# Float64 weights to float32: sign kept by a one-source mask on 16-bit halves

## The chip, the cores and the metric

The kernel runs on one core of one Trainium2 chip. The metric is the device time of one execution in microseconds (us), lower is better. Engines are named as in the profile: PE (matrix engine), PEld (its weight loads), DVE (vector engine), ACT (scalar engine), POOL (GpSimd), SP (issues the DMAs).

## What is computed

```python
A = sm(q, k_lm); Bm = sm(q_lm, k_lm); C = sm(q_lm, k)     # landmark attention, 4 batches x 8 heads
Z = Bm.T / (norm1 * norminf + 1e-6)
for _ in range(6): Z = 2 * Z - Z @ Bm @ Z
x = A @ Z @ C @ v                                         # 2304 tokens x 512
h = x @ w_in;  x = (h * sigmoid(h)) @ w_out               # first MLP, 512 -> 2048 -> 512
xn = x / rms(x) * rms_g                                   # second MLP, 512 -> 1536 -> 512
return (silu(xn @ w_gate) * (xn @ w_val)) @ w_out2
```

The five weight matrices arrive as float64 and are used as pairs of float32 values (a leading part and a remainder), so that each product is three matmuls.

## The kernel before

The program has two large parts. In the first, four batches go through attention and the first MLP; in the second, six blocks of 384 tokens, taken in pairs, go through the second MLP, whose weights have been prepared during the first part and kept in DRAM.

A float64 value is two 32-bit words. The high word holds sign, 11 exponent bits and 20 mantissa bits, the low word the other 32 mantissa bits. A float32 needs the sign, 8 exponent bits and 23 mantissa bits, so 20 mantissa bits come from the high word and 3 from the top of the low word. `to_f32` does this in four instructions per piece (512 or 1024 values in each of 128 partitions):

- L164, ACT: reads the high word as a float32, takes its absolute value and scales it by 2^-112, which moves the exponent; result in `c`.
- L165, ACT: reads the upper 16 bits of the low word and turns them into the three missing bits, an integer 0 to 7, written over the low word as int32.
- L169, DVE: ANDs the high word with the sign bit and ORs the three bits in; result over the low word.
- L171, DVE: shifts `c` left by 3 and ORs the low word in; `c` is now the float32.

It is a generator that yields ahead of each DVE instruction, so callers can spread it. Raw tiles are called `winr` (`w_in`), `wor` (`w_out`) and `r_v`, `r_g`, `r_o` (second MLP); results are `win`, `wos` and `c_v`, `c_g`, `c_o`. Results `wos`, every other `c_` tile and the evacuated sums `e` share one pool of four buffers (`stage`); L164 is the instruction that needs such a buffer, L165 needs only the raw tile. There are 8 `win` loads (those for the first 1024 columns in two pieces of 512 each), 16 `wor` loads and 36 loads for the second MLP, 64 pieces of each instruction in all.

After that a result of `w_out` is split into leading part and remainder (`split`, L145 to L148; the leading part of the first four by DVE on L147, later by ACT on L145, the remainder by POOL on L148).

The order of the work is made by a scheduler from program order and priorities. At the start the attention of batch 0 for its two groups of heads runs step by step, and the string `CONV` says how many conversion steps are let in behind each attention step. When attention is done, `wprime` (L428 to L431) multiplies the attention's small matrices with `win` and splits the result (`wp`); `moe1_h` (L587, L590) multiplies that with the queries' side and applies silu; `moe1_out` (L599) multiplies with `w_out` into four accumulators `a`; `moe1_sum` (L609, L611) moves the accumulators out to `e`, and the next half of the batch takes their place. From step 24 of the MLP loop on, `conversion` works through the second MLP's weights. Each engine runs its own list strictly in order.

Of the kernel before, what the change touches and what calls it, by code (L numbers as in the profile page):

```python
# [13 lines left out]
U16 = mybir.dt.uint16  # L14
AF = mybir.ActivationFunctionType
ALU = mybir.AluOpType
# [44 lines left out]
def nystrom_moe_kernel(ctx: ExitStack, tc: tile.TileContext, q, k, v, w_in, w_out, w_gate, w_val, w_out2, rms_g, out):  # L61
    nc = tc.nc
    PE, DVE, ACT, POOL, SP = nc.tensor, nc.vector, nc.scalar, nc.gpsimd, nc.sync
# [90 lines left out]
    def to_f32(c, raw, act=1024, dve=1024):  # L154


        n = c.shape[1]
        w = raw.rearrange("p (f t) -> p f t", t=2)
        lo, hi = w[:, :, 0], w[:, :, 1]
        lo16 = raw.bitcast(U16).rearrange("p (f t) -> p f t", t=4)[:, :, 1]  # L160
        ci = c.bitcast(I32)
        for x in range(0, n, act):
            y = slice(x, min(n, x + act))
            ACT.activation(c[:, y], hi[:, y].bitcast(F32), AF.Abs, scale=2.0 ** -112)  # L164
            ACT.activation(lo[:, y], lo16[:, y], AF.Copy, scale=2.0 ** -13, bias=2.0 ** -14 - 0.5)  # L165
        for x in range(0, n, dve):
            y = slice(x, min(n, x + dve))
            yield
            DVE.scalar_tensor_tensor(out=lo[:, y], in0=hi[:, y], scalar=-0x80000000, in1=lo[:, y], op0=ALU.bitwise_and, op1=ALU.bitwise_or)  # L169
            yield  # L170
            DVE.scalar_tensor_tensor(out=ci[:, y], in0=ci[:, y], scalar=3, in1=lo[:, y], op0=ALU.logical_shift_left, op1=ALU.bitwise_or)  # L171

    def finish(gn):
        for _ in gn:
# [11 lines left out]
    def load_win(n, g):  # L186
        raw = wslot(f"winr_{g}_{n}", [P, 2, 1024], I32)
        SP.dma_start(out=raw, in_=win_v[g, n].rearrange("c p f -> p c f"))
        yield
        t = nslot(2 * n + g, f"win_{g}_{n}", [P, 2, 512])  # L190
        size = (512, 512) if n < 2 else (1024, 1024)
        yield from to_f32(t.rearrange("p c f -> p (c f)"), raw.rearrange("p c f -> p (c f)"), *size)
        win_t[g, n] = t

    def load_wout(f):
        raw = wslot(f"wor_{f}", [P, 2 * DM], I32, f"o{f}", 1)
        SP.dma_start(out=raw, in_=w_out_v[f * P:(f + 1) * P, :])
        yield
        s = stage(f"wos_{f}")
        yield from to_f32(s, raw)  # L200
        t = wslot(f"wo_{f}", [P, 2, DM], F32R, f"o{f}", 1)
        split(t, s, lo=POOL, hi=DVE if f in range(EARLY) else ACT)
        wo_t[f] = t
# [255 lines left out]
    def conversion():  # L459

        raws, gens, outs = {}, {}, {}

        def load(n, f, what):
            raw = raws[n] = nslot(4 + n % 3, f"r_{what}_{f}", [P, 1024], I32)
            if what == "o":
                SP.dma_start(out=raw, in_=w_out2_v[f * P:(f + 1) * P, :])
            else:
                src = w_gate_v if what == "g" else w_val_v
                SP.dma_start(out=raw.rearrange("p (k f) -> p k f", k=KD), in_=src[:, f * 2 * P:(f + 1) * 2 * P].rearrange("(k p) f -> p k f", p=P))

        def start(n, f, what):
            outs[n] = stage(f"c_{what}_{f}") if n % 2 else nslot(7, f"c_{what}_{f}", [P, 512])
            gens[n] = to_f32(outs[n], raws[n])
            next(gens[n])

        def go_on(n):
            next(gens[n], None)

        def store(n, f, what):
            j = "vgo".index(what)  # L480
            SP.dma_start(out=w2d[f, :, j * 512:(j + 1) * 512], in_=outs[n])

        jobs = []
        for n, (f, what) in enumerate((f, what) for f in PRE + list(range(PRE_N, NF2)) for what in "vgo"):
            jobs += [(4 * n + 1, load, n, f, what), (4 * n + 9, start, n, f, what), (4 * n + 10, go_on, n), (4 * n + 11, go_on, n), (4 * n + 15, store, n, f, what)]
        return in_time(jobs)
# [368 lines left out]
    t = 0  # L855
# [203 lines left out]
```

## Time and profile before

| what | us |
|---|---|
| three runs | 896.09, 898.78, 899.06 |
| median | 898.78 |
| profiled execution, first to last instruction (its span) | 890.5 |
| PE busy in it | 831.2 |
| DVE busy | 538.4 |
| ACT busy | 453.0 |
| POOL busy | 206.8 |

The profile gives the span of the profiled execution and no separate time for it; the three runs lie 5.6 to 8.6 us above the span. A row of the stretch view gives the busy time of each engine between two moments of the span, then the clock granted to PE as a share of full speed (1.00 is the 2.4 GHz level, 0.50 the 1.2 GHz level). A row of the timeline gives start, length, engine, line, operation, output<-input, shape, and in brackets the idle time before it with what ended it.

### The profile page before, as it was taken

The numbers are of one execution on the slowest core, as the hardware profiler recorded it, in microseconds if no ns is written. First come the engines' busy times: TensorE is split into PE (matmuls) and PEld (weight loads), VectorE is DVE, ScalarE is ACT, GpSimd is POOL, SyncE is SP. The second block draws the span as 40 slices with busy tenths as digits, with TensorE's granted clock in tenths as the row PEclk, the third lists the DMA queues.
The fourth block names the chain that finished last, engine by engine and source line by source line (L and its number), as shares of the span: only waits on it lengthen the run. The fifth ranks groups of instructions, "written<-read, shape, count | busy, mean of one in ns | idle before, by whom it ended". The sixth has DMA issues, their size and how long they took to land.

```text
span 890.5 us, 14692 instructions
## 1 busy us (share of the span) xinstructions
PE 831.2 (93%) x5436; PEld 747.6 (84%) x5436; DVE 538.4 (60%) x1070; ACT 453.0 (51%) x926; POOL 206.8 (23%) x232
## 2 busy tenths in 40 slices
PE   4578999999989999999899999999999999999996
PEld 3447788688868888899899988999989999999995
DVE  5988978448954665668873568843468534333332
ACT  2858784468446955657363445533445433222322
POOL 5257563223322333372650002400000000000000
PEclk9659999999999999999999999999999999999998
DMA  9774935883868556979668545759655556655553
GB/s 326 284 287 145 307 111 186 285 269 108 275 201 286 157 159 240 361 276 290 242 241 313 211 168 191 248 213 318 249 213 211 206 201 240 230 200 194 205 194 71
DMA packets 72584, 202.82 MB, mean 228 GB/s; under 512 B 6592, under 2 KB 34240, under 8 KB 68544
## 3 DMA queue, kind: packets, MB, share of 16 engines
q1 hardware_dynamic: 72512, 201.88, 64.7%
q8 instruction: 43, 0.70, 0.3%
q14 instruction: 29, 0.24, 0.1%
HBM read 149.29 MB, written 52.56 MB: 227 GB/s over the span
## 4 chain that ended last, share of the span: by engine, by line
PE 55%; DVE 9%; DMA 9%; ACT 8%; issue 4%; POOL 1%; SPq 0%; DVEq 0%; ACTq 0%; POOLq 0%
PE ga L737 16%; PE o L811 16%; PE gc L737 8%; PE a L599 7%; PE gb L737 4%; PE h L587 3%; DMA r_g<-in_moe_w_gate_dram 2%; DMA w7d<-w7p 2%; DMA wod<-wop 2%; DMA r_o<-in_moe_w_out_dram 1%; DMA r_v<-in_moe_w_val_dram 1%; DVE w7p L148 1%; DVE kT L217 1%; DVE qT L217 1%; DMA win<-wind 1%
## 5 line engine op out<-in xcount | busy, mean ns | idle before, releaser
L599 PE MATMUL a<-hl,wo 128*128 128x288 f32 x1536 | 228.2, 297 | 10.8 <-DVE e L611 6.7
L599 PEld LDWEIGHTS a<-hl,wo 128*128 128x128 f32 x1536 | 212.6, 190 | 14.7 <-DVE e L611 4.8
L811 PE MATMUL o<-oc,u 128*128 128x512 f32 x648 | 178.1, 393 | 0.0
L737 PE MATMUL ga<-x,w 128*128 128x384 f32 x840 | 170.6, 337 | 1.1 <-ACT a L217 1.0
L737 PEld LDWEIGHTS ga<-x,w 128*128 128x128 f32 x840 | 150.5, 188 | 14.2 <-ACT a L217 2.3
L587 PE MATMUL h<-at,wp 128*128 128x288 f32 x768 | 134.4, 310 | 8.1 <-DVE wp L431 4.1
L587 PEld LDWEIGHTS h<-at,wp 128*128 128x128 f32 x768 | 111.3, 194 | 32.8 <-issue 10.7
L811 PEld LDWEIGHTS o<-oc,u 128*128 128x128 f32 x648 | 119.3, 188 | 13.0 <-DVE u L148 0.3
L148 POOL TENSOR_TENSOR hl<-s,hl 128x288 fp32r<-128x288 f32 x86 | 78.0, 912 | 155.4 <-ACT hl L145 107.4
L217 DVE TENSOR_TENSOR v<-u,gc 128x384 f32<-128x384 f32 x72 | 39.7, 552 | 119.5 <-PE gc L737 116.1
L737 PE MATMUL gc<-x,w 128*128 128x384 f32 x420 | 84.6, 336 | 0.0
L590 ACT ACTIVATE s<-h 128x288 f32<-128x288 f32 x128 | 52.0, 409 | 50.8 <-PE h L587 35.8
L737 PEld LDWEIGHTS gc<-x,w 128*128 128x128 f32 x420 | 74.6, 188 | 3.1
L217 DVE TENSOR_TENSOR u<-z,v 128x384 f32<-128x384 f32 x72 | 40.4, 561 | 50.5 <-ACT z L217 49.5
L217 ACT COPY u<-ga 128x384 f32<-128x384 f32 x72 | 34.5, 480 | 70.3 <-PE ga L737 70.0
L145 ACT CAST u<-u 128x384 fp32r<-128x384 f32 x72 | 36.9, 513 | 65.3 <-DVE u L217 65.2
L148 DVE TENSOR_TENSOR u<-u,u 128x384 fp32r<-128x384 f32 x72 | 40.1, 557 | 28.3 <-ACT u L145 28.0
L502 POOL TENSOR_TENSOR t<-fw 128x256 f32<-128x256 f32 x24 | 23.7, 1005 | 144.4 <-ACT x L701 82.8
L145 ACT CAST hl<-s 128x288 fp32r<-128x288 f32 x128 | 54.8, 433 | 2.4
L217 ACT ACTIVATE z<-ga 128x384 f32<-128x384 f32 x36 | 17.7, 492 | 73.2 <-PE ga L737 73.1
L737 PE MATMUL gb<-x,w 128*128 128x384 f32 x210 | 42.3, 336 | 0.9 <-DVE v L217 0.9
L737 PEld LDWEIGHTS gb<-x,w 128*128 128x128 f32 x210 | 36.7, 188 | 1.4 <-DVE v L217 1.2
(166 smaller groups left out, 1050.3 us busy)
## 6 DMA issues: line engine op xcount, KB each, us to landing
w<-w7d SPq DMA_DIRECT2D x31, 1792.0 KB, 7.3
oc<-wod SPq DMA_DIRECT2D x32, 512.0 KB, 8.0
win<-wind SPq DMA_DIRECT2D x20, 512.0 KB, 6.6
fw<-w2d SPq DMA_DIRECT2D x12, 768.0 KB, 6.8
winr<-in_moe_w_in_dram SPq DMA_DIRECT2D x8, 1024.0 KB, 10.7
wor<-in_moe_w_out_dram SPq DMA_DIRECT2D x16, 512.0 KB, 8.1
w7d<-w7p SPq DMA_DIRECT2D x16, 512.0 KB, 5.3
r_v<-in_moe_w_val_dram SPq DMA_DIRECT2D x12, 512.0 KB, 5.4
```

The costliest lines, as they stand in the source:

```text
L145: ACT.copy(dst[:, 0], src)
L148: lo.tensor_tensor(dst[:, 1], src, dst[:, 0].bitcast(F32), op=ALU.subtract)
L217: self.last = getattr(self.eng, name)(*args, **kw)
L502: POOL.tensor_tensor(t[:, to], x, y, op=ALU.subtract)
L587: PE.matmul(ph, w[:, x, fo:fo + P], a[:, y, tk], start=i == 0, stop=i == 5)
L590: ACT.activation(s, ph, AF.Silu)
L599: PE.matmul(acc[d], w[:, x, d * P:(d + 1) * P], hl[:, y], start=start and i == 0, stop=stop and i == 2)
L737: mm[0] = PE.matmul(acc, w7[:, x, o, kk], xs[:, y, kk], start=start and n == 0, stop=stop and n == 5, skip_group_check=True)
L811: PE.matmul(oacc[n], hls[j][:, x, t * P:(t + 1) * P], w[:, y], start=f == 0 and i == 0, stop=f == NF2 - 1 and i == 2)
```

## The change

The sign is no longer moved into the low word. L169 becomes a one-source instruction that masks the upper 16-bit half of the high word in place with 0x8000, so only the sign bit stays there. L165 writes its three bits as a 16-bit number into the lower half of the same high word. The high word then holds sign and three bits, and L171 ORs it in instead of the low word.

```diff
-        lo, hi = w[:, :, 0], w[:, :, 1]
-        lo16 = raw.bitcast(U16).rearrange("p (f t) -> p f t", t=4)[:, :, 1]
+        hi = w[:, :, 1]
+        q = raw.bitcast(U16).rearrange("p (f t) -> p f t", t=4)
...
             ACT.activation(c[:, y], hi[:, y].bitcast(F32), AF.Abs, scale=2.0 ** -112)
-            ACT.activation(lo[:, y], lo16[:, y], AF.Copy, scale=2.0 ** -13, bias=2.0 ** -14 - 0.5)
+            ACT.activation(q[:, y, 2], q[:, y, 1], AF.Copy, scale=2.0 ** -13, bias=2.0 ** -14 - 0.5)
...
-            DVE.scalar_tensor_tensor(out=lo[:, y], in0=hi[:, y], scalar=-0x80000000, in1=lo[:, y], op0=ALU.bitwise_and, op1=ALU.bitwise_or)
+            DVE.tensor_scalar(q[:, y, 3], q[:, y, 3], 0x8000, None, op0=ALU.bitwise_and)
...
-            DVE.scalar_tensor_tensor(out=ci[:, y], in0=ci[:, y], scalar=3, in1=lo[:, y], op0=ALU.logical_shift_left, op1=ALU.bitwise_or)
+            DVE.scalar_tensor_tensor(out=ci[:, y], in0=ci[:, y], scalar=3, in1=hi[:, y], op0=ALU.logical_shift_left, op1=ALU.bitwise_or)
```

Both L165 and L169 now overwrite what L164 reads. Before, L165 and L169 needed only the raw tile; now both stand behind L164. L169 no longer needs L165, and L171 needs all three.

The scheduler makes a new order of this. PE's list is the same but for three places where neighbouring matmuls change places. The other lists differ wherever a conversion stands. Three places follow.

First, ACT at the end of batch 0's attention, where the first `w_out` pieces are converted (`wor` raw, `wos` result, L430 the leading part of `wp`):

```order
-L165 ACTIVATE wor_4_561<-wor_4_561 128x512
-L165 ACTIVATE wor_5_563<-wor_5_563 128x512
-L165 ACTIVATE wor_6_565<-wor_6_565 128x512
-L165 ACTIVATE wor_7_567<-wor_7_567 128x512
 L430 CAST wp_0_0_532<-pw_0_0_0_533 128x512
 L164 ACTIVATE wos_4_573<-wor_4_561 128x512
-L165 ACTIVATE wor_8_581<-wor_8_581 128x512
+L165 ACTIVATE wor_4_561<-wor_4_561 128x512
 L430 CAST wp_0_0_532<-pw_0_0_1_534 128x512
 L164 ACTIVATE wos_5_583<-wor_5_563 128x512
-L165 ACTIVATE wor_9_591<-wor_9_591 128x512
+L165 ACTIVATE wor_5_563<-wor_5_563 128x512
```

The L165 of pieces 4 to 7 ran ahead of their L164; now each follows its own.

Second, DVE where the first half of batch 0 ends and its accumulators are moved out (L611; `kT` and `lm` belong to the attention of batch 1, `winr_3` and `win_3` are the last two `w_in` loads). Before:

```order
L169 SCALAR_TENSOR_TENSOR wor_680<-wor_680 128x512
L217 TENSOR_REDUCE kT_0_780<-kT_0_780 128x2x32
L169 SCALAR_TENSOR_TENSOR wor_778<-wor_778 128x512
L217 TENSOR_TENSOR lm_1_0_974<-kT_0_780,m_95 128x64 x2
L169 SCALAR_TENSOR_TENSOR winr_3_761<-winr_3_761 128x1024
L171 SCALAR_TENSOR_TENSOR win_3_1036<-win_3_1036,winr_3_761 128x1024
L611 COPY e_0_0_0_890<-a_0_0_0_656 128x288
L169 SCALAR_TENSOR_TENSOR winr_3_768<-winr_3_768 128x1024
L611 COPY e_0_0_2_896<-a_0_0_2_658 128x288
L171 SCALAR_TENSOR_TENSOR win_3_1041<-win_3_1041,winr_3_768 128x1024
```

The same place on DVE now:

```order
L217 TENSOR_TENSOR lm_0_930<-qT_0_730,m_95 128x64
L169 TENSOR_SCALAR winr_3_761<-winr_3_761 128x1024
L171 SCALAR_TENSOR_TENSOR win_3_1036<-win_3_1036,winr_3_761 128x1024
L611 COPY e_0_0_0_890<-a_0_0_0_656 128x288
L169 TENSOR_SCALAR winr_3_768<-winr_3_768 128x1024
L171 SCALAR_TENSOR_TENSOR win_3_1041<-win_3_1041,winr_3_768 128x1024
L611 COPY e_0_0_2_896<-a_0_0_2_658 128x288
L217 TENSOR_REDUCE kT_0_780<-kT_0_780 128x2x32
L431 TENSOR_TENSOR wp_2_912<-pw_2_0_913,wp_2_912 128x512
```

Two masks and the reduction of `kT` no longer stand ahead of the first L611; the last L171 now stands ahead of the second.

Third, ACT in the attention of batch 1, first group (`sa`, `bb`, `ec` are exponentials, `s` silu; each change between them loads a table). Before:

```order
L217 ACT_TABLE_LOAD
L217 ACTIVATE sa_0_1003<-sa_0_1003 128x576
L590 ACT_TABLE_LOAD
L590 ACTIVATE s_1_6_1070<-h_1_6_1063 128x288
L217 ACT_TABLE_LOAD
L217 ACTIVATE bb_0_1129,su_0_1130<-c_1_0_1055,nb_0_1088 128x32
```

The same place on ACT now:

```order
L217 ACT_TABLE_LOAD
L217 ACTIVATE sa_0_1003<-sa_0_1003 128x576
L217 ACTIVATE bb_0_1129,su_0_1130<-c_1_0_1055,nb_0_1088 128x32
L217 ACTIVATE ec_0_1128,su_0_1130<-c_1_0_1055,nb_0_1088 128x8x32
L217 ACTIVATE ec_0_1128,su_0_1130<-c_1_0_1054,nb_0_1088 128x10x32
L145 CAST wo_1051<-wos_1046 128x512
L590 ACT_TABLE_LOAD
L590 ACTIVATE s_1_6_1070<-h_1_6_1063 128x288
```

Silu no longer comes between the exponentials here, which takes out two loads; the second group of the same batch gains two, and the first group of batch 3 loses two (24 loads before, 22 now).

## Rows read from the trace of the kernel before

**Rows 1.** The page, parts 1 and 2: busy times, then tenths in 40 slices.

```profile
PE 831.2 (93%) x5436; PEld 747.6 (84%) x5436; DVE 538.4 (60%) x1070; ACT 453.0 (51%) x926; POOL 206.8 (23%) x232
...
PE   4578999999989999999899999999999999999996
...
PEclk9659999999999999999999999999999999999998
```

**Rows 2.** Stretches: length; PE, PEld, DVE, ACT, POOL busy (instructions); clock; DMA share; GB/s.

```profile
25.00:50.00 25.00, 16.40 (x152) 10.72 (x153) 24.57 (x74) 16.99 (x32) 6.61 (x6) 0.58 0.83 315
50.00:75.00 25.00, 20.39 (x118) 15.81 (x117) 18.69 (x23) 17.82 (x33) 17.90 (x14) 0.73 0.46 172
75.00:100.00 25.00, 21.22 (x149) 17.88 (x147) 24.28 (x30) 19.37 (x38) 14.41 (x12) 0.93 0.76 264
100.00:125.00 25.00, 22.15 (x203) 17.98 (x202) 21.13 (x51) 21.80 (x44) 13.47 (x13) 1.00 0.58 184
125.00:350.00 225.00, 214.47 (x1803) 187.84 (x1802) 143.81 (x353) 135.24 (x286) 68.42 (x76) 0.99 0.65 209
...
465.00:890.50 425.50, 415.69 (x2156) 384.01 (x2156) 204.72 (x381) 162.65 (x322) 14.53 (x13) 0.99 0.59 215
```

**Rows 3.** Lines L169, L147, L165: ns min/median/max; then who waited for L169.

```profile
L169 DVE SCALAR_TENSOR_TENSOR wor<-wor x16: 678/684/1794, 44.9 to 113.3; 128x512 int32<-128x512 int32 x16
...
  PEld h L587: 1.7, 1
...
L147 DVE CAST wo<-wos x4: 415/417/769, 46.9 to 54.0; 128x512 fp32r<-128x512 f32 x4
...
L165 ACT ACTIVATE wor<-wor x16: 646/672/719, 38.4 to 112.6; 128x512 int32<-128x512 uint16 x16
```

**Rows 4.** Timeline of DVE ahead of the first product of batch 0's MLP.

```profile
50.72 1.75 DVE L169 SCALAR_TENSOR_TENSOR wor<-wor 128x512 int32<-128x512 int32 x1
...
53.43 0.69 DVE L431 TENSOR_TENSOR wp<-pw,wp 128x512 fp32r<-128x512 f32 x1
54.04 0.77 DVE L147 CAST wo<-wos 128x512 fp32r<-128x512 f32 x1
```

**Rows 5.** Timeline of POOL in the same stretch.

```profile
50.33 1.59 POOL L148 TENSOR_TENSOR wo<-wos,wo 128x512 fp32r<-128x512 f32 x1 [1.62 <-ACT wor L165]
52.94 1.59 POOL L148 TENSOR_TENSOR wo<-wos,wo 128x512 fp32r<-128x512 f32 x1 [1.02 <-DVE wo L147]
```

**Rows 6.** Timeline of PE: its waits, and one undisturbed row for comparison.

```profile
38.79 1.19 PE L390 MATMUL pe<-rt,ebd 128*128 128x128 f32 x4 [1.23 <-DVE rt L217]
...
54.18 1.81 PE L587 MATMUL h<-at,wp 128*128 128x288 f32 x6 [3.30 <-DVE wp L431]
...
79.10 1.74 PE L599 MATMUL a<-hl,wo 128*128 128x288 f32 x12
...
89.22 2.59 PE L599 MATMUL a<-hl,wo 128*128 128x288 f32 x12 [2.94 <-DVE e L611]
...
110.16 1.06 PE L587 MATMUL h<-at,wp 128*128 128x288 f32 x6 [0.90 <-ACT s L590]
...
114.64 0.91 PE L369 MATMUL ct<-ident,ec 128*96 128x128 f32 x6 [1.35 <-ACT s L590]
...
149.34 1.84 PE L599 MATMUL a<-hl,wo 128*128 128x288 f32 x12 [1.37 <-DVE e L609]
```

**Rows 7.** Timeline of DVE where the first accumulators are moved out.

```profile
80.50 2.29 DVE L217 TENSOR_REDUCE kT<-kT 128x64 f32<-128x1152 f32 x1
...
85.74 1.21 DVE L169 SCALAR_TENSOR_TENSOR winr<-winr 128x1024 int32<-128x1024 int32 x1
...
88.72 0.44 DVE L611 COPY e<-a 128x288 f32<-128x288 f32 x1
```

**Rows 8.** Timeline of ACT: a wait for a stage buffer, and a table load.

```profile
56.61 0.67 ACT L164 ACTIVATE wos<-wor 128x512 f32<-128x512 f32 x1 [1.36 <-POOL wo L148]
...
108.40 1.28 ACT L590 ACT_TABLE_LOAD   x1
```

## The prediction, made before the changed kernel was run

> **What bounds the kernel now.** I read the page first, then the stretch view, then the timelines of the stretches where PE idles. PE is busy for 831.2 of 890.5 us [rows 1], so 59 us of idle time and the time lost at a low clock are all that a cheaper conversion can touch. In the second MLP, from 465 us on, PE works 415.69 of 425.5 us and no conversion runs there [rows 2]: nothing can change. From 125 to 350 us, where the 36 pieces of the second MLP's weights are converted, PE is idle 225 - 214.47 = 10.5 us with DVE and ACT each busy less than two thirds of the time [rows 2]. The dense losses are early: from 25 to 50 us DVE is busy 24.57 of 25 us and PE 16.40, at a granted clock of 0.58 [rows 2]. There DVE sets the pace: PE waits for DVE in the iterations of attention, as in the row with 1.23 us [rows 6], and the first product of the MLP waits 3.30 us for `wp` from L431 on DVE [rows 6]. A second loss stands at 89.22 us, where PE waits 2.94 us for the accumulators that L611 moves out on DVE [rows 6], and the clock over that stretch is 0.93 [rows 2]. A third lies at 110 to 115 us, 0.90 and 1.35 us of waiting for silu on ACT [rows 6].
>
> **The cost of the mask.** The two-source L169 takes 0.684 us for 512 values, and up to 1.794 us [rows 3]. The trace of before has no one-source pass on 16-bit halves. The bounds: the cast L147, one source in SBUF, 512 values, takes 0.417 us [rows 3]; a pass at the pace of L169 would take 0.684. I take 0.42, since L147 shares with the mask what L169 does not have: a single source in SBUF. So each piece of 512 saves 0.684 - 0.417 = 0.27 us, and one of 1024 about twice that. Below 0.417 I have no row; if it went lower still the gains below grow by at most as much again, which the low end of the range covers.
>
> The longest L169s are not slow arithmetic. The one at 50.72 us took 1.75 us while POOL worked from 50.33 to 51.92 [rows 4, 5], and the one-source L147 at 54.04 took 0.77 instead of 0.417 while POOL worked until 54.53 [rows 3, 4, 5]. So a mask started beside POOL waits too, and I give no gain for that wait. The Trainium skill, in "SBUF — State Buffer", section "SBUF: two separate sides", states the rule behind this: DVE and GpSimd hold a shared port pair for a whole instruction, and an instruction of DVE in a two-port mode is locked out as one with two SBUF sources is. It speaks against the hope that dropping a source frees DVE from POOL; the stretched L147 agrees. Were the mask free of it, the piece at 50.72 alone would save 1.75 - 0.42 = 1.3 us instead of 0.27.
>
> L165 keeps its 0.672 us [rows 3]: it already reads 16-bit numbers at that spacing, only the output changes its width. L164 and L171 stay. So ACT's work is the same and DVE loses 60 x 0.27 + 4 x 0.53 = 18 us of 538.4 [rows 1]; what counts is where.
>
> **Stretch up to the first product, 25 to 54 us.** Eleven L169 of 512 values stand in DVE's list there. At 0.27 each that is 2.9 us, and DVE is nearly never idle, so most of it moves L431 forward. I take off about 0.3 for one that stands in a gap where DVE waits for PE anyway, and 0.6 for the places where POOL's instruction, not the mask, ends the wait (rows 5 show two such POOL instructions of 1.59 us). That leaves 2.0 us earlier for the product at 54.18 [rows 6]. Bounds: 1.1 (the four masks of `wor` alone, if attention's own round trips through PE hide the others) and 2.9. New waits here: L171 now needs L165, but ACT has done the `winr` and first `wor` pieces two or more us before DVE comes to them, and the L165 that now follow the L164 of pieces 5 to 7 stand where ACT sits idle for a stage buffer, 1.36 us before the L164 at 56.61 [rows 8]. 0.67 fits into that. So I cost the new order of ACT at nothing here; if that cover were gone it would be 2 x 0.67 = 1.3 us on the way to the first silu.
>
> **The accumulators, 84 to 92 us.** Before, the first L611 at 88.72 stood behind a mask of 1.21 us at 85.74 and its L171, and these behind a reduction of 2.29 us and two other masks [rows 7]. PE waited 2.94 us, and the twelve matmuls after it took 2.59 instead of 1.74 us [rows 6]. The clock of 0.93 over 25 us is 1.75 us lost in all [rows 2]. So 4.7 us lie here. In the new list the reduction and two masks are gone from ahead of the first L611, 2.29 + 2 x 0.68 = 3.6 us of DVE work, but the second L611 stands behind a L171, which in turn needs ACT's last L165. I expect the first accumulator to come free about 3 us earlier and the third about 1.5 us earlier than now; PE needs the third after six matmuls. I take -1.5 us. Bounds: -4.7 (the wait and the slow clock both go; at 149.34 a wait of 1.37 us left the twelve matmuls at 1.84, close to 1.74 [rows 6]) and +3.0 (see the second rival).
>
> **Table loads, 100 to 130 us.** The first group of batch 1 loses two loads of 1.28 us [rows 8], against waits of 0.90 + 1.35 us for silu [rows 6]; the second group gains two. I take 0 for the pair, with bounds of 2.25 either way.
>
> **Second MLP's weights, 125 to 350 us.** 36 masks save 36 x 0.27 = 9.7 us of DVE, but PE waited directly for a L169 only 1.7 us in one place [rows 3]. L165 behind L164 makes each conversion a little longer from stage buffer to result, with loads far ahead. I take 0, bounds -1.7 and +1.7. After 350 us, 0.
>
> **Sum.** -2.0 - 1.5 + 0 + 0 = -3.5 us, so a span of 890.5 - 3.5 = 887.0. The three runs lie 5.6 to 8.6 us above the profiled span; against the median the same difference gives 898.78 - 3.5 = 895.3 us.
>
> **Rivals.**
> First, the early gain is eaten: PE comes 1 to 2 us earlier to the accumulators and waits that much longer there, since their release hangs on transfers and ACT. Then -2.0 + 1.5 = -0.5 is left, 898.3 us. For it: DVE is busy 24.28 of 25 us in that stretch [rows 2], so PE's earliness alone moves nothing. Against it: the list ahead of the first L611 is shorter.
>
> Second, slower: the second L611 stands behind a L171 that now waits for ACT's L165 of the last `winr` piece. Everything behind it on DVE is queued too: the reduction of `kT`, `wp` of the next columns, the exponentials' maxima; PE waits for the accumulator. If that L165 ends later than 88.7 us, where the first L611 stands now [rows 7], each us costs PE one. At 5 us late (about the present wait and the twelve slow matmuls behind it once more, 2.94 + 2.59) and with the early gain kept, the sum is -2.0 + 5.0 = +3.0, so 901.8 us.
>
> Third, the change doesn't do what it says: the mask runs at one value a cycle, 0.684 us like L169. Then DVE saves nothing in the first stretch, only the new order acts: -1.5 by the accumulators, 897.3 us. In its favour, no row shows a 16-bit operand on DVE. The Trainium skill, "VectorE: DVE Perf Modes", section "Mode 1× (REGULAR) — the baseline", names odd strides as what falls back to it; its section on the 2×_2P mode asks only for SBUF and an even length, which the mask has. By the one it would be this rival, by the other my forecast; the trace cannot tell.
>
> **How the numbers follow.** A measurement of this kernel can tell about 0.3%, 2.7 us, from no change. Forecast: 0.53 (both gains, 892 to 896). Eaten gain: 0.20. Slower by the L611: 0.12. Slow mask: 0.10. A small rest, 0.05, for gains well beyond (the wait and the slow clock at 89 us both gone, -2.9 - 4.7, 891.2). For the range I take that low end, 891.0, and on the high side I go past no change to 900.0, which leaves out the second rival. Faster by over 0.3% (below 896.1): 0.50 of the forecast and the small rest, 0.55. Within 0.3%: the first and third rivals and 0.03 of the forecast, less 0.02, 0.31. Slower: the second rival and those 0.02, where the first rival's wait grows past the gain, 0.14.
>
> **What would show it.** In the profile after, L169 should read a median near 0.42 us for 512 values; 0.68 makes the third rival right. The first product of the MLP should start near 52.2 us. The wait for L611 should be under 2 us and the stretch 75 to 100 us should have a clock nearer 1.00; a longer wait there, with L171 of `win_3` just ahead of L611, is the second rival. Table loads should number 22. L165 should keep 0.67 us. I am wrong if a 16-bit write costs more than that, or if from 125 us on PE's idle time grows beyond 10.5 us by more than 2.

## The result and the profile after

The changed kernel takes 909.1 us (median of 4 runs, 905.2 to 909.8) against 897.4 us for the kernel before on the same chip: a ratio of 1.0144, 95% interval 1.0108 to 1.0180. It is slower by 12 to 13 us (the medians differ by 11.7, the ratio gives 12.9) where 3.5 us of gain were forecast, 895.3 us in a range of 891.0 to 900.0. The profiled execution spans 908.0 us, with a mean granted clock of 0.962 (before 890.5 and 0.973).

The two spans differ by 17.5 us, more than the medians. The kernel before has a fourth run now, 892.17 us. It lies 1.7 us above the span of 890.5, as the changed kernel's 909.75 lies 1.75 above 908.0, so it is most likely the profiled one: the stretches below hold the quickest run of before against the longest of after.

The page's busy times of after, to be held against [rows 1]:

```profile
PE 836.8 (92%) x5436; PEld 751.9 (83%) x5436; DVE 541.2 (60%) x1070; ACT 491.8 (54%) x924; POOL 202.8 (22%) x232
```

ACT works 491.8 - 453.0 = 38.8 us more, though it has no new instruction. DVE, which was to lose 18 us, has gained 2.8. The stretch view of after, with the columns of [rows 2]:

```profile
25.00:50.00 25.00, 16.27 (x146) 11.22 (x150) 23.42 (x70) 20.13 (x28) 5.46 (x4) 0.50 0.73 272
...
75.00:100.00 25.00, 18.44 (x126) 16.40 (x126) 19.54 (x21) 21.40 (x32) 12.65 (x11) 0.86 0.69 228
100.00:125.00 25.00, 20.77 (x144) 16.02 (x141) 22.84 (x45) 22.00 (x38) 13.97 (x13) 0.95 0.64 227
125.00:350.00 225.00, 206.81 (x1765) 180.54 (x1764) 139.53 (x347) 151.70 (x278) 64.88 (x74) 0.98 0.63 200
```

PE loses 21.22 - 18.44 = 2.8 us of work between 75 and 100 us, 1.4 between 100 and 125 us, and 214.47 - 206.81 = 7.7 us between 125 and 350 us, the stretch that the prediction counted at nothing. In the same stretch ACT is 151.70 - 135.24 = 16.5 us busier.

The groups of L165 and L169 (instructions: shortest/median/longest in ns, first and last start, forms) say where ACT's time comes from:

```profile
L165 ACT ACTIVATE wor<-wor x16: 1328/1368/1447, 40.5 to 135.4; 128x512 uint16<-128x512 uint16 x16
L165 ACT ACTIVATE winr<-winr x12: 1321/1406/2553, 20.8 to 90.6; 128x512 uint16<-128x512 uint16 x8, 128x1024 uint16<-128x1024 uint16 x4
L165 ACT ACTIVATE r_v<-r_v x12: 1342/1368/1452, 123.2 to 356.7; 128x512 uint16<-128x512 uint16 x12
...
L169 DVE TENSOR_SCALAR wor<-wor x16: 703/768/1846, 46.7 to 130.3; 128x512 uint16<-128x512 uint16 x16
L169 DVE TENSOR_SCALAR winr<-winr x12: 725/738/1548, 22.3 to 90.7; 128x512 uint16<-128x512 uint16 x8, 128x1024 uint16<-128x1024 uint16 x4
```

L165 takes twice its time, 1.37 us instead of 0.67 [rows 3]. The mask reads 0.74 to 0.77 us, more than the two-source instruction that it replaces (0.684 [rows 3]).

A row's length is not the time for which it holds up the next instruction. Two rows of DVE before, with the instruction behind L169, then the same after:

```profile
37.54 0.68 DVE L169 SCALAR_TENSOR_TENSOR winr<-winr 128x512 int32<-128x512 int32 x1
38.14 0.28 DVE L217 TENSOR_TENSOR ebd<-pe,mask 128x128 f32<-128x128 f32 x1
```

```profile
37.43 0.73 DVE L169 TENSOR_SCALAR winr<-winr 128x512 uint16<-128x512 uint16 x1
37.95 0.31 DVE L217 TENSOR_TENSOR ebd<-pe,mask 128x128 f32<-128x128 f32 x1
```

The next instruction starts 0.60 us behind L169 before and 0.52 us behind the mask. So DVE's list gains less than 0.1 us from a mask where 0.27 was forecast, while an instruction that needs the mask's result waits longer than before. On ACT, over the L165 of 512 values with no idle time behind them, the next instruction starts 0.57 us (median) behind L165 before and 1.11 us behind it now, 0.54 us more.

And the new wait, L171 for L165, is in the trace; the view of L171 lists what its engine waited for in us and how often:

```profile
  ACT r_v L165: 6.5, 7
  ACT wor L165: 6.3, 4
  ACT winr L165: 5.8, 4
  ACT r_o L165: 5.5, 9
  ACT r_g L165: 5.4, 9
```

29.5 us in 33 places, all on DVE. Three timelines show the place of the second rival, batch 0's accumulators, on PE, ACT and DVE:

```profile
90.86 0.67 PE L599 MATMUL a<-hl,wo 128*128 128x288 f32 x3 [3.00 <-DVE e L611]
93.72 2.53 PE L599 MATMUL a<-hl,wo 128*128 128x288 f32 x9 [2.18 <-ACT e L611]
```

```profile
90.58 2.55 ACT L165 ACTIVATE winr<-winr 128x1024 uint16<-128x1024 uint16 x1
...
93.19 0.77 ACT L611 COPY e<-a 128x288 f32<-128x288 f32 x2
```

```profile
89.21 1.23 DVE L171 SCALAR_TENSOR_TENSOR win<-win,winr 128x1024 int32<-128x1024 int32 x1 [1.26 <-ACT winr L165]
90.36 0.45 DVE L611 COPY e<-a 128x288 f32<-128x288 f32 x1
90.72 1.55 DVE L169 TENSOR_SCALAR winr<-winr 128x1024 uint16<-128x1024 uint16 x1
93.17 1.23 DVE L171 SCALAR_TENSOR_TENSOR win<-win,winr 128x1024 int32<-128x1024 int32 x1 [0.89 <-ACT winr L165]
94.31 0.45 DVE L611 COPY e<-a 128x288 f32<-128x288 f32 x1
```

The last L165 of `winr` holds ACT until 93.1 us. Behind it stand ACT's own share of the copies L611 and, on DVE, L171 and the next L611. The first L611 on DVE is late in the same way: the L171 ahead of it waits 1.26 us for the L165 of the other last `winr` piece. PE waits 3.00 + 2.18 us where it waited 2.94 [rows 6].

### The profile page after: what moved, and what is told of

The parts are those of the page before. It is cut to its first block, busy times and chain, and to the rows that moved or that the text cites. A ratio compares the mean times of both kernels' runs of the same rounds, so it can differ in the third digit from the quotient of the medians.

```text
span 908.0 us, 14711 instructions
## 1 busy us (share of the span) xinstructions
PE 836.8 (92%) x5436; PEld 751.9 (83%) x5436; DVE 541.2 (60%) x1070; ACT 491.8 (54%) x924; POOL 202.8 (22%) x232
## 4 chain that ended last, share of the span: by engine, by line
PE 50%; DMA 8%; DVE 7%; ACT 5%; issue 2%; SPq 0%; ACTq 0%; DVEq 0%
PE ga L737 16%; PE o L811 15%; PE gc L737 8%; PE a L599 4%; PE gb L737 4%; DMA w7d<-w7p 3%; PE h L587 2%; DMA wod<-wop 1%; DVE w7p L148 1%; DMA fw<-w2d 1%; PE pw L428 1%; DMA win<-wind 1%; DVE x L702 1%; DMA x2T<-e 1%; DMA w2d<-c_g 0%
## 5 line engine op out<-in xcount | busy, mean ns | idle before, releaser
L599 PE MATMUL a<-hl,wo 128*128 128x288 f32 x1536 | 229.6, 298 | 12.9 <-DVE e L611 5.4
L148 DVE TENSOR_TENSOR hl<-s,hl 128x288 fp32r<-128x288 f32 x42 | 32.6, 786 | 9.2 <-ACT hl L145 8.9
```

Source lines behind the costliest of these rows:

```text
L148: lo.tensor_tensor(dst[:, 1], src, dst[:, 0].bitcast(F32), op=ALU.subtract)
L599: PE.matmul(acc[d], w[:, x, d * P:(d + 1) * P], hl[:, y], start=start and i == 0, stop=stop and i == 2)
```

## The experiments

Three theories stood at the start. A: the doubled L165 carries the loss, and what doubles it is the write of 2-byte numbers 8 bytes apart (A1). B: the 16-bit mask on DVE. C: the new order, with L165 and L169 behind L164 and done in place. Each row below compares with the kernel before on the same chip.

| run | what differs from before | us | ratio, 95% interval |
|---|---|---|---|
| e1_act16 | L165 as changed; two-source mask | 920.98 | 1.0281 (1.0262 to 1.0300) |
| e2_mask16 | 16-bit mask; L165 as before; three bits left out | 901.41 | 1.0076 (1.0050 to 1.0102) |
| e3_inplace | result of L169 in the high word | 894.70 | 0.9986 (0.9965 to 1.0006) |
| e5_dose | L165 writes 16 bits, all 64 | 907.55 | 1.0154 (1.0137 to 1.0170) |
| e6_dose_late | the same, late 36 alone | 903.59 | 1.0124 (1.0103 to 1.0144) |
| e9_dose_early | the same, early 28 alone | 896.96 | 1.0018 (0.9993 to 1.0042) |
| e7_mask32 | 32-bit mask; L165 as before; three bits left out | 888.75 | 0.9945 (0.9924 to 0.9966) |
| e8_after32 | the changed kernel with a 32-bit mask | 913.04 | 1.0218 (1.0203 to 1.0233) |
| e10_bits_dve | late bits by DVE | 902.33 | 1.0081 (1.0050 to 1.0113) |
| e11_bits_pool | late bits by POOL | 904.82 | 1.0098 (1.0070 to 1.0125) |
| e13_bits_dve_late | late bits by DVE, one step later | 901.25 | 1.0052 (1.0028 to 1.0077) |
| e14_bits_dve_all | all bits by DVE | 910.49 | 1.0166 (1.0144 to 1.0188) |
| e12_no_bits | 32-bit mask, no L165; three bits left out | 882.55 | 0.9854 (0.9829 to 0.9878) |

**One half of the change at a time.** First ACT's half, then DVE's, then a part of the order alone. In all three L171 also ORs in the high word, a line that the diffs leave out.

```diff
-ACT.activation(lo[:, y], lo16[:, y], AF.Copy, ...)
-DVE.scalar_tensor_tensor(out=lo[:, y], in0=hi[:, y], scalar=-0x80000000, in1=lo[:, y], and, or)
+ACT.activation(q[:, y, 2], q[:, y, 1], AF.Copy, ...)
+DVE.scalar_tensor_tensor(out=hi[:, y], in0=hi[:, y], scalar=-0x7ffffff9, in1=hi[:, y], and, and)
```

> L165 writes 16-bit as in the changed kernel; the sign pass on DVE is again a 32-bit instruction with two sources (it reads the high word twice and keeps sign and the three bits). Theory A (ACT's 16-bit write, 1.37 us instead of 0.67 for 512 values, is what costs): L165 stays at 1.37, L169 about 0.68, time 1.0 to 1.7% above the kernel before. Theory B (the mask on 16-bit halves costs, 0.75 instead of 0.68): within 0.4% of before. Theory C (the new order, L165 and L169 behind L164, costs): 1.0 to 1.7% above, since the dependencies are those of the changed kernel.

```diff
-DVE.scalar_tensor_tensor(out=lo[:, y], in0=hi[:, y], scalar=-0x80000000, in1=lo[:, y], and, or)
+DVE.tensor_scalar(q[:, y, 3], q[:, y, 3], 0x8000, None, op0=ALU.bitwise_and)
```

> L165 writes 32 bits into the low word as before; the mask is the 16-bit one of the changed kernel. Left out: the three low bits (L171 ORs in what is in the high word), so L171 does not wait for L165. Theory A: L165 0.67, L169 0.75, time within 0.5% of before. Theory B: 1% or more above before. Theory C: L169 stands behind L164, part of the loss stays, 0.5 to 1.5% above.

```diff
-DVE.scalar_tensor_tensor(out=lo[:, y], in0=hi[:, y], ...)
+DVE.scalar_tensor_tensor(out=hi[:, y], in0=hi[:, y], ...)
```

> The instructions of the kernel before with their sizes; only the sign pass writes sign and bits into the high word instead of the low word, so it stands behind both L164 and L165. Theory A and B: within 0.4% of before. Theory C: 1% or more above before.

Of C, what e3 tests falls: writing into the high word, with L169 behind L164, cost nothing that could be measured (0.9986). L165 behind L164, the other half of C, is in no run by itself, since in e3 L165 still writes the low word. The mask alone (e2, 1.0076) lost less than its theory B wanted and lies in the range that was expected for C; e7 below tells these apart. A is too large: with L165 at 1.39 us the time came out above that of the full change. One wait in it is longer than in the changed kernel. In e1 the mask stands behind L165, and the view of L169 adds up to 76 us of waiting for it; in the changed kernel the mask runs ahead of L165. So the runs are not halves of one sum, and the dose runs below keep the lists fixed.

**What doubles it.** Behind the last product of the kernel before, 17 forms of 512 values each were run four times with PE and POOL at rest.

> The kernel before, with 17 forms of the two instructions four times each behind the last product, on tiles of their own, POOL at rest; the output is not touched. Sixteen-bit values stand 8 bytes apart where not said otherwise. Theory A1 (a 16-bit element written apart costs ACT a second step): 16-bit writes 8 bytes apart 1.37 us, also from a float32 source and as bfloat16; dense 16-bit writes 0.67; 32-bit writes 0.67. Theory A2 (it is the pair 16-bit in and 16-bit out of the same word): 1.37 only in place, 0.67 into another tile. Theory A3 (any 16-bit output costs double): 1.37 dense too. For DVE: in-place mask 8 bytes apart about 0.74; on 32-bit words 8 bytes apart 0.42 if only the width stands in the way of two values a cycle, 0.68 if the spacing does; dense 16-bit 0.28 to 0.42.

The groups view of that tail (output<-input, busy us and mean ns). On ACT, L1053 writes int32 8 bytes apart, L1054 16-bit numbers 8 bytes apart in the same tile, L1055 the same into another tile, L1056 dense, L1057 4 bytes apart; L1059 reads float32 and writes 2-byte integers 8 bytes apart (L1061, the same as bf16, reads 1335 ns too). On DVE, L1062 is the changed mask, L1063 the mask on 32 bits in place, L1064 dense, L1066 reads 8 bytes apart and writes dense, L1067 reads dense and writes 8 bytes apart, L1068 is the 32-bit mask dense, L1069 the two-source L169.

```profile
L1055 ACT ACTIVATE by<-bx 128x512 uint16<-128x512 uint16 x4 | 5.6, 1405 | 0.0
L1054 ACT ACTIVATE bx<-bx 128x512 uint16<-128x512 uint16 x4 | 5.6, 1392 | 0.0
L1059 ACT ACTIVATE by<-bz 128x512 uint16<-128x512 f32 x4 | 5.3, 1335 | 0.1
...
L1057 ACT ACTIVATE by<-bx 128x512 uint16<-128x512 uint16 x4 | 3.1, 774 | 0.1
L1062 DVE TENSOR_SCALAR bw<-bw 128x512 uint16<-128x512 uint16 x4 | 2.9, 737 | 6.2 <-ACT bw L1034 6.1
L1067 DVE TENSOR_SCALAR bz<-bw 128x512 uint16<-128x512 uint16 x4 | 2.9, 734 | 0.1
L1069 DVE SCALAR_TENSOR_TENSOR bw<-bw 128x512 int32<-128x512 int32 x4 | 2.8, 694 | 0.1
L1056 ACT ACTIVATE by<-bx 128x512 uint16<-128x512 uint16 x4 | 2.6, 654 | 0.1
...
L1053 ACT ACTIVATE bx<-bx 128x512 int32<-128x512 uint16 x4 | 2.6, 652 | 0.0
...
L1063 DVE TENSOR_SCALAR bw<-bw 128x512 int32<-128x512 int32 x4 | 1.7, 429 | 0.1
L1066 DVE TENSOR_SCALAR bz<-bw 128x512 uint16<-128x512 uint16 x4 | 1.7, 427 | 24.2 <-ACT by L1061 24.1
L1068 DVE TENSOR_SCALAR bw<-bw 128x512 int32<-128x512 int32 x4 | 1.7, 427 | 0.1
L1064 DVE TENSOR_SCALAR bw<-bw 128x512 uint16<-128x512 uint16 x4 | 1.2, 294 | 0.1
```

A1 holds on both engines. Reading 16-bit numbers 8 bytes apart is cheap (0.65 on ACT, 0.43 on DVE, L1053 and L1066). Writing them 8 bytes apart is dear: 1.34 to 1.41 us on ACT, where source, type and tile move it by 5% at most, and 0.73 on DVE. At 4 bytes apart it is 0.77 and 0.45 (L1065), dense 0.65 and 0.29. On DVE the 32-bit word at that spacing costs no more than a dense one (L1063, L1068); on ACT it costs what the dense 16-bit write costs (L1053, L1056), a dense 32-bit one was not run. POOL was at rest, so work on POOL is not the cause.

**L165's price alone, lists fixed.** In the kernel before, only the width of L165's output changes; it goes over the upper half of the low word. Every engine's list stays as it was, instruction for instruction. Then the same for the late and the early pieces apart.

```diff
-ACT.activation(lo[:, y], lo16[:, y], AF.Copy, ...)
+ACT.activation(lo16[:, y], lo16[:, y], AF.Copy, ...)
```

> The kernel before with one edit: L165 writes its result as a 16-bit number over the upper half of the low word instead of as a 32-bit number over the whole low word. Every engine's list is the same as before, instruction for instruction, so only the duration of L165 differs. (The three bits land 16 places too high and the low half of the low word is not cleared, so the weights are a few per cent off; no work is left out.) Theory A (the doubled time of L165 is what costs, whatever the order of the lists): L165 reads 1.34 to 1.41 us for 512 values, ACT is busy 38 us more, PE waits longer for ACT and for DVE behind L165, and the time is 0.8 to 1.6% above the kernel before, 903 to 910 us. Rival D (ACT has room, busy 453 of 890 us; the loss of the changed kernel comes from L171 waiting for three instructions and from the new lists): within 0.3% of the kernel before.

> As the run with the 16-bit write in all 64 L165, but only the 36 of the second MLP's weights (r_v, r_g, r_o, from 115 us on) write 16 bits; the 28 of w_in and w_out stay as in the kernel before. Lists again the same as before on every engine. My prediction counted this stretch at nothing, with bounds of 1.7 us either way. Theory A with the loss spread over both: +2 to +8 us. If the early pieces carry all of it: within 0.3% (2.7 us) of the kernel before, and then the part from 125 us on was rightly counted at nothing.

> The other half of the run with the 16-bit write in the second MLP's pieces alone: here the 28 L165 of w_in and w_out write 16 bits over the upper half of the low word, the 36 of r_v, r_g and r_o stay as in the kernel before. Lists the same as before on every engine. (The early weights are a few per cent off; no work is left out.) If the two halves add up (all 64 gave 1.0154, the late 36 gave 1.0124): 1.002 to 1.005. If what the early half loses is partly taken back in the late half when both are slow: 1.006 to 1.01, since alone it has all its loss to itself.

All 64 give 1.0154, as much as the whole change. The late 36 alone give 1.0124, the early 28 alone 1.0018, which is not told from nothing. The two add up within their intervals. This answers the dispute between theory A and rival D: ACT, busy 453 of 890 us, had no room for it, with every list as before. The stretch view of the late dose, then its group `r_v`:

```profile
125.00:350.00 225.00, 207.01 (x1739) 180.70 (x1738) 139.96 (x350) 151.61 (x280) 65.55 (x74) 1.00 0.63 200
```

```profile
L165 ACT ACTIVATE r_v<-r_v x12: 1348/1366/1407, 115.5 to 332.6; 128x512 uint16<-128x512 uint16 x12
```

PE works 207.01 us there, against 214.47 before and 206.81 in the changed kernel. A sum over a fixed window also holds what reached it late: e9, whose late L165 are unchanged, reads 210.03 there. The same matmuls tell it better. The first 100 us are as before, and the loss sits in many small waits. Three of PE's in the late dose, each on ACT (start, length, and in brackets the wait and its releaser), then the same three before:

```profile
118.49 0.71 PE L276 MATMUL pq<-qT,lm 128*64 128x288 f32 x4 [1.71 <-ACT ct L217]
...
169.91 0.53 PE L587 MATMUL h<-at,wp 128*128 128x288 f32 x2 [2.00 <-ACT wp L430]
...
307.37 0.71 PE L276 MATMUL pq<-qT,lm 128*64 128x288 f32 x4 [1.99 <-ACT ct L217]
```

```profile
117.14 0.71 PE L276 MATMUL pq<-qT,lm 128*64 128x288 f32 x4 [0.50 <-ACT ct L217]
...
165.91 0.53 PE L587 MATMUL h<-at,wp 128*128 128x288 f32 x2 [1.40 <-ACT wp L430]
...
299.95 0.71 PE L276 MATMUL pq<-qT,lm 128*64 128x288 f32 x4 [0.35 <-ACT ct L217]
```

The three start 1.35, 4.00 and 7.42 us later than before. Attention's steps on ACT stand behind a L165 twice as long. ACT ahead of the first of the three, in the late dose, then before:

```profile
116.62 1.43 ACT L165 ACTIVATE r_g<-r_g 128x512 uint16<-128x512 uint16 x1
117.76 0.94 ACT L217 COPY ct<-ct 96x512 f32<-96x512 f32 x2
```

```profile
115.94 0.68 ACT L165 ACTIVATE r_g<-r_g 128x512 int32<-128x512 uint16 x1
116.49 0.86 ACT L217 COPY ct<-ct 96x512 f32<-96x512 f32 x2
```

**The mask's width alone, lists fixed.** e7 differs from e2 in the width of L169 and in nothing else; their lists are the same on every engine.

```diff
-DVE.tensor_scalar(q[:, y, 3], q[:, y, 3], 0x8000, None, op0=ALU.bitwise_and)
+DVE.tensor_scalar(hi[:, y], hi[:, y], -0x80000000, None, op0=ALU.bitwise_and)
```

> L165 as in the kernel before (32 bits over the low word, 0.67 us); L169 masks the whole high word in place with one 32-bit one-source instruction; L171 ORs the high word in. The three low bits are left out of the weights, no instruction is. Its lists are those of the run with the 16-bit mask on every engine, so the two differ only in the width of the mask. Theory B (the 16-bit mask's 0.72 us is a part of the loss): L169 reads 0.43 us, DVE is busy about 18 us less than with the 16-bit mask, and the time falls from 1.0076 of the kernel before to 0.995 to 1.002. If it is under 0.997, the idea of a one-source mask would have paid had it run at 0.43. Rival (the 0.76% comes from the new lists, with L169 and L171 behind L164): it stays at 1.005 to 1.01 though the mask takes 0.43.

```profile
L169 DVE TENSOR_SCALAR wor<-wor x16: 416/422/1516, 45.9 to 122.7; 128x512 int32<-128x512 int32 x16
```

```profile
75.00:100.00 25.00, 24.17 (x178) 20.56 (x177) 22.85 (x33) 22.16 (x42) 14.98 (x14) 1.00 0.87 299
```

The mask takes 0.42 us, the value that the prediction had assumed, and the time goes from 1.0076 to 0.9945: 16.5 us of DVE's work (542.6 to 526.1 busy) are worth about 1.3%, 11.7 us. Between 75 and 100 us PE works 24.17 us instead of 21.22 in the kernel before, at a clock of 1.00 instead of 0.93. PE's rows, first product and accumulators:

```profile
54.19 1.81 PE L587 MATMUL h<-at,wp 128*128 128x288 f32 x6 [2.79 <-DVE wp L431]
...
87.07 0.66 PE L599 MATMUL a<-hl,wo 128*128 128x288 f32 x3 [0.60 <-ACT e L611]
87.95 1.06 PE L599 MATMUL a<-hl,wo 128*128 128x288 f32 x6 [0.23 <-ACT e L611]
```

The wait at the accumulators has shrunk from 2.94 to 0.83 us, but the first product starts where it did (54.18 [rows 6]). So one of the forecast's two gains exists, and with a dear mask it does not come; the other did not come even at 0.42 us. This kernel is no replacement, since it leaves the three bits out.

> The changed kernel with one edit: the mask is one 32-bit one-source instruction on the high word in place, which keeps the sign and the three bits, so it stands behind L165. L169 should read 0.43 us instead of 0.77. L165 stays at 1.37. Theory A: the time stays well above the kernel before; the DVE time saved (64 times 0.3 us) is given back since L169 now waits for L165 as L169 did before the change; 1.010 to 1.025. Rival (the 16-bit mask is what costs the changed kernel): within 0.4% of the kernel before.

```diff
-DVE.tensor_scalar(q[:, y, 3], q[:, y, 3], 0x8000, None, op0=ALU.bitwise_and)
+DVE.tensor_scalar(hi[:, y], hi[:, y], -0x7ffffff9, None, op0=ALU.bitwise_and)
```

With the three bits the cheap mask must follow L165, since it now covers the half that L165 writes. It takes 0.43 us, DVE is busy 17 us less than in the changed kernel, and the time is higher, 1.0218. L169 waited 76 us for L165, as in e1 (23.2 us for `r_g`, 21.6 for `r_o`, 17.4 for `r_v`, 7.4 for `winr`, 6.6 for `wor`). By these two runs, whose lists differ in some places too, masking ahead of L165 gives the changed kernel more than the width of its mask costs it.

That wait is not the whole of it. In e5 L169 stands behind a dear L165 too, and waits 54 us (39 before), and the time is 1.0154 against 1.0281 in e1. What e1 has beyond e5 is that L165 stands behind L164 and L169 writes the high word (with the new lists of that), and e3 found the second free. So at the doubled price L165 behind L164 is the likely cost; no run shows it by itself.

**Is it ACT, or any engine?** Three exact kernels (no bit is left out) take the late L165 away from ACT; the fourth does so for all pieces.

```diff
-ACT.activation(lo[:, y], lo16[:, y], AF.Copy, ...)
+DVE.tensor_scalar(lo[:, y], lo[:, y], 29, None, op0=ALU.logical_shift_right)     # e10, e13, e14
+POOL.tensor_scalar(lo[:, y], lo16[:, y], 2.0 ** -13, 2.0 ** -14 - 0.5, op0=ALU.mult, op1=ALU.add)   # e11
```

> The opposite dose, exact: in the 36 pieces of the second MLP the three bits come from DVE, a 32-bit one-source shift of the low word by 29 in place (0.43 us by the forms measured), and L165 on ACT is gone there; L169 and L171 as before, early pieces as before. ACT loses 36 x 0.68 = 24.5 us, DVE gains 36 x 0.43 = 15.5. If ACT is what sets the pace from 115 us on, as the doubled L165 suggests (25 us more on ACT cost 11 us): 2 to 6 us faster than the kernel before, 0.993 to 0.998. If only added work hurts and the list of before has cover for what is there: within 0.3%. If DVE sets the pace there: slower by up to 4 us.

> As the run with the shift on DVE, but POOL computes the three bits of the 36 late pieces with L165's own arithmetic (multiply, add, rounded to int32 over the low word). POOL is busy 68 of the 225 us there; I take 0.9 us for each, from its 899 ns for L148 of 288 values, up to 1.6. ACT loses 24.5 us, DVE keeps its work, but instructions of DVE that start beside POOL's are held up. If ACT sets the pace: 0.993 to 0.999. If POOL's hold on DVE costs as much as ACT gains: 0.998 to 1.004. If L148 on POOL, which makes the remainders that PE waits for, is pushed back: slower, up to 1.01.

> As the run with the shift on DVE in the 36 late pieces, with the shift one step later, right ahead of the piece's L169, so that DVE no longer stands waiting for the load of the raw tile (DVE waited 29 us for loads of r_g and r_o in front of the shift). Exact. If that wait in DVE's strictly ordered list was the loss: ACT works 24.5 us less, DVE 15.5 us more, and L169 no longer waits for ACT; 0.992 to 0.999. If added work on DVE costs there by itself: 1.002 to 1.008.

> The same for all 64 pieces: no L165 on ACT at all, a shift of 0.43 us on DVE ahead of each L169. Exact. In the early stretch DVE is busy 24.57 of 25 us, so 11 shifts of 0.43 us ahead of the first product should push it back by up to 4.7 us: 1.002 to 1.01 there, less whatever the late pieces gain. If it is not slower than with the late pieces alone, L169's and L171's waits for ACT were worth the added DVE work early too.

All four are slower than before. Something else is mixed in: the instruction that makes the bits is the one that waits for the load of the raw tile. Before, ACT waited 26.2 us for loads of `r_v`, `r_g` and `r_o` in front of L165. In e10 DVE waits for them, 15.1 us for `r_g` and 14.0 for `r_o`, and in e11 POOL, 30.5 us. In e13, with the shift one step later, DVE still does (L168 is the shift there; us in total, times, longest):

```profile
DVE r_g L168 <- DMA r_g<-in_moe_w_gate_dram: 15.8, 7, 4.5
DVE r_o L168 <- DMA r_o<-in_moe_w_out_dram: 11.2, 5, 3.3
```

So e13 did not do what its expectation wanted, and 1.0081 and 1.0052 are not told apart by their intervals. In e13 DVE is busy 15.2 us more and ACT 21.6 us less, and the time is higher; whether the added work on DVE or the wait that moved to DVE's list costs it stays open. POOL took 0.66 us for its bits (0.9 was estimated), and e11 lost 1%. In e14 DVE is busy 25.00 of 25 us from 75 to 125 us, and its 1.0166 is beyond what was expected. The lists of these kernels are new ones, so the price of the order is in these numbers too. What they do show is that none of the ways tried was cheaper than L165 on ACT.

> The run with the 32-bit mask once more, now with L165 left out altogether (the three low bits were not used there, but L165 still ran). It bounds what any cheaper way to the three bits could gain on top: ACT loses 64 x 0.68 = 44 us, no instruction takes its place, and the lists are made anew, PE's too. If ACT sets the pace where the second MLP's weights are converted: 0.98 to 0.99. If ACT's room before was real and only additions hurt: as the run with the mask alone, 0.991 to 0.998.

Without L165 the time falls from 0.9945 to 0.9854, and PE works 25.00 of the 25 us between 75 and 100 us (24.17 in e7).

So ACT's 0.67 us for the bits was not free either; with nothing put in its place and new lists, its absence is worth 8 us (this leaves the three bits out, as e7 does). No exact kernel of this study is measurably faster than the one before.

## Why the prediction was wrong

- **"L165 keeps its 0.672 us ... only the output changes its width."** This step failed. It measured 1.37 us, and in the lists of before that alone costs 1.54% (e5), as much as the whole change. The rows of before held one L165, one that reads 16 bits and writes 32; the width of the write was what changed, and its cost was never bounded from above. The prediction bounded the mask from both sides and this not at all. It did say that it would be wrong if a 16-bit write cost more than 0.67.
- **"I take 0.42" for the mask.** Failed: 0.74 to 0.77. The row L147 shares the single source, but writes 4-byte numbers. The upper bound, 0.684, was too low as well. With the lists fixed the width costs 1.3% (e7 against e2). The third rival had the right side, but not the time: with such a mask and L165 at 0.67 it gave 897.3 us, below the kernel before, and e2 took 1.0076 of it. DVE's next instruction starts no later behind an undisturbed mask than behind L169, so the mask's pace alone does not explain what e2 loses against the kernel before (DVE busy 542.6 against 538.4); new lists, later results and masks beside POOL are left, and no run parts them. The Trainium skill, "VectorE: DVE Perf Modes", section "Mode 2×_2P — use both read ports for one tensor", asks for SBUF and an even length. Both masks of e4 meet that, and the 32-bit one read 0.43 us, the 16-bit one 0.74, so it does not tell them apart. The Trainium skill, on the same page, section "Mode 1× (REGULAR) — the baseline", names odd strides among what falls back to it; the 32-bit mask at the same spacing read 0.43, so the spacing alone does not force the slow pace.
- **First product 2.0 us earlier.** Failed: it starts at 55.92 instead of 54.18, 1.7 us later. PE is that late already when attention is done (L428 at 48.21 instead of 46.50), and its wait for `wp` behind that is alike (3.23 us against 3.30), so the time is lost in attention's iterations. One place is at 32.38 us, where PE waits 1.37 us for DVE and waited for nothing before. The cheap mask did not help: in e7 the product starts at 54.19, with a wait of 1.14 us at that place. So, with the new lists, the step that eleven cheaper masks move L431 forward failed by itself, beside the mask's cost; which change in DVE's list ate the gain is not shown. That a one-source mask is held up by POOL was forecast and held (one at 52.51 us took 1.80 us).
- **Accumulators, -1.5 us.** Failed: the second rival's mechanism came true in its place. The L165 of the last `winr` piece ended at 93.1 us, 4.4 us past the rival's point of 88.7. Its price of 5 us was too high: from the end of the last product ahead of the wait to the end of the twelve matmuls behind it PE took 8.39 us instead of 5.53, 2.9 more. The price counted the twelve slow matmuls at their whole 2.59 us, though they are only 0.85 us over the 1.74 of undisturbed ones. The first accumulators of the second half were copied out at 126.26 instead of 119.00, 7.3 us later; beyond the 1.7 and the 2.9 half of the rest arose at about 120 us, where PE waited 2.79 us for silu on ACT (1.35 before [rows 6]). Where the mask does take 0.42 us and L165 0.67 (e7), the wait is nearly gone, as the forecast wanted.
- **Second MLP's weights, 0 with bounds of 1.7 us.** Failed, the largest term that was missing. PE did 7.7 us less work there (at the same place of its list it is 7.3 us late at 125 us and 17.1 at 350), and the late dose alone shows why: 36 longer L165 make ACT 21.5 us busier (474.5 against 453.0) and cost 1.24%, 11 us, though ACT is busy only 135.24 of 225 us [rows 2]. "DVE and ACT each busy less than two thirds of the time" was taken for room. It was not: the conversions share strictly ordered lists with attention's steps, and a longer one delays whatever stands behind it.
- **Table loads, 0.** The count is the forecast 22. What the new places of the loads give or cost in waits was not separated from the longer L165.
- **L165 behind L164 costs nothing.** Not tested at L165's old price: e3 puts only L169 behind L164 (0.9986). At the doubled price e1 against e5 speaks against it.

What stays open: how the 12 to 13 us divide between L165 and the mask in the changed kernel. L165 alone gives 1.54% in the lists of before. Taken the other way, from e7 (0.9945) the mask's width gives 1.3% on fixed lists and leads to e2 (1.0076), and L165 with its new place and L171's wait for it gives the remaining 0.7% to 1.0144. The two costs overlap, and which is the larger depends on which is there first. That both come from the one thing, 16-bit numbers written 8 bytes apart, is shown by e4.

## What to carry to other kernels

Before narrowing an operand, price the write by itself: measure it in its own spacing, on each engine whose output narrows, even where the instruction and its source stay the same. A share of two thirds is no room where an engine's list is in strict order and holds steps that others wait for; double the cost of one group with the order unchanged, and read what a microsecond there is worth. To judge one factor where a scheduler remakes the lists, find the edit that leaves every list as it is.

## What the runs showed of the hardware

- A write of 2-byte numbers 8 bytes apart takes ACT 1.34 to 1.41 us for 512 values against 0.65 for 4-byte numbers at the same spacing; 4 bytes apart it is 0.77, dense 0.65. Source, type and tile change it by 5% at most (e4).
- On DVE the same write takes 0.73 us with one source against 0.43 for 4-byte numbers and 0.29 dense; reading at that spacing and writing dense takes 0.43 (e4).
- One-source 32-bit masks and shifts 8 bytes apart in SBUF read 0.42 to 0.43 us for 512 values, against 0.69 for the two-source form (e4, e7, e10).
- The next instruction can start ahead of a row's end: 0.60 us behind the start of the two-source form, 0.52 behind the 16-bit mask though its row is longer (0.73 against 0.68), and 0.33 behind the 32-bit mask (36.59 to 36.92 us in e7).
